# Leftover columns in four groups of 32 partitions, and the column products of k and k+8 made together

## The chip, the cores and the metric

The kernel runs on one core of one Trainium2 chip. The metric is the device time of one execution in microseconds, the median of several runs. An execution is recorded by the hardware profiler; the profile is a page of summaries and a trace of single instructions. The engines are PE (TensorE; PEld is its weight load), DVE (VectorE), ACT (ScalarE), POOL (GpSimd) and SP (the queue that issues most DMAs).

## What is computed

```
def _A_ref(x, w_r, w_i):                     # x: 1 x 2048 x 576
    X = rfft2(x, axes=(-2, -1))
    X = X * (w_r + 1j * w_i)                 # w: 2048 x 289
    return irfft2(X, s=(2048, 576)).astype(bfloat16)

def _B_ref(x, w_gate, w_up, w_down):         # 576 x 4608, 4608 x 576
    return (gelu(x @ w_gate) * (x @ w_up)) @ w_down

h  = x + _A_ref(layernorm(x), w_r, w_i)
h2 = h + _B_ref(layernorm(h), w_gate, w_up, w_down)
```

All arrays are bfloat16. The first part is a spectral filter, the second a gated feed-forward network.

## The kernel before

The order of every engine's work is the order in which the program is written (a manual schedule); waits between engines are put in from what each instruction reads and writes. All sums in PSUM share one pool of four slots, each of two banks (`two`), so a product can start only when the slot that it gets has been evicted.

**Row stage.** The 2048 rows lie as 128 partitions times 16 values of h. For each h, DVE makes a 128-point Fourier table that already holds the row's 1/sigma (`norms`, L391: `FR` from `F16` and `rstd`; half of it with plus, half with minus sign). `row16` (L318) multiplies the columns of x with it: columns d and d+288 are added with both signs, so a group of 128 columns gives 128 sums and 128 differences, and a further product with the constant `mneg` takes the mean away. Two groups cover columns 0 to 255 and 288 to 543. The 2 x 32 columns left over, 256 to 287 and 544 to 575, go through `row16_rest` (L347) in two halves of 64 columns, unfolded: 64 x 128 products, two for the data and two for the mean per h, for four h at a time (`rests`). ACT or DVE moves everything from PSUM to `Bt` (`evict`, L361; `evict4`, L367), five groups of 128 partitions by 2048 values: 0 and 2 are sums, 1 and 3 differences, 4 the leftovers. Before the first product, `fill` (L313) runs 12 products of 512 columns whose result is not used. In parallel the Fourier table of the columns, `DT`, is made by POOL, DVE (`phases`, `mirror`) and ACT (`col_sin`); `DF` is a copy of its third group that is zero outside the two leftover strips.

**Column stage.** It runs in turns, one per pair of row frequencies k and k+8, in the order 1, 2, ... 7, 0. `f2(c)` (L543) makes the column products of one of the two, six products of 128 x 290: per parity two on `Bt` and `DT` and one on the leftovers with `DF`. `f2_out` (L560) brings them to SBUF on ACT (`pq`). `f3` (L570) combines the two by eight products, which ACT evicts to `g` and `hs`. DVE adds and subtracts these (`sum_of`, L595), multiplies with the filter's weights (`wmul`, L607: L618 products, L623/L624/L638/L639 sums) and leaves `Zt`; `i3` (L646) makes the way back by ten products per pair, evicted by ACT to `EO`. A turn i holds `f2` of pair i, `f3` of pair i-1, `wmul` of pair i-2 with the sums of pair i-1 inside it, `f2` of the second half of pair i, and `i3` of pair i-3. The loop reads, cut:

```
for i in range(n + 1):
    if not last: f2(order[i]); f2_out(order[i])         # if i != 1
    ...
    f3(order[i-1], 0); f3(order[i-1], 1)
    ...
    wmul(order[i-2], i-1, order[i-1])
    if not last and i: f2(order[i] + 8); f2_out(order[i] + 8)
    ...
    for s in range(3): i3(order[i-3], s)
```

**After it.** `inv_cols` (L703) makes the columns' way back from `EO` with `DQ`, a copy of `DT` in blocks of 58 that `load_dq` (L512) puts together by DMA; `add_rows` (L838) makes the rows' way back, and then comes the feed-forward network: `gate` (L972, products L978) and the down products (L1021, L1040), on weights that SP loads ahead.

Of the kernel before, what the change touches and what calls it, by code (L numbers as in the profile page):

```python
# [20 lines left out]
P = 128  # L21
# [21 lines left out]
def kernel_body(  # L43
# [67 lines left out]
    DF = keep.tile([P, 2, 2, JH], BF16, name="DF")  # L111
# [28 lines left out]
    def minus_means(lo, hi):  # L140
        sh = [P, 2, hi - lo]
        G.tensor_tensor(
            mneg[:, :, lo:hi],
            mv[:, lo:hi, 0].unsqueeze(1).to_broadcast(sh),
            neg[:].unsqueeze(2).to_broadcast(sh),
            ALU.mult,
        )
# [40 lines left out]
    V.memset(DF[:], 0.0)  # L188
# [18 lines left out]
    iota(iD[64:128, 2:3], [[0, 1]], 2 * P + 64 + 192, 1)  # L207
# [103 lines left out]
    FILL = {0: 12}  # L311

    def fill(dst, n):  # L313

        for _ in range(n):
            T.matmul(dst, lhsT=ident[:], rhs=h_sb[:, 0, 0:512], start=True, stop=True)

    def row16(h):  # L318
        if h % 2 == 0:
            ps_f[h] = two("f2t")  # L320
        f2t, b = (ps_f[h], 0) if h in ps_f else (ps_f[h - 1], 1)
        fill(f2t[:, b, :], FILL.get(h, 0))
        x = h_sb[:, h, :]
        plus = FR[:, h, 0:1, :].to_broadcast([P, 2, P])
        for t in range(2):
            for n, d0 in ((0, t * P), (1, DH + t * P)):
                T.matmul(  # L327
                    f2t[:, b, t * 2 * P : (t + 1) * 2 * P],
                    lhsT=x[:, d0 : d0 + P],
                    rhs=FR[:, h] if n else plus,  # L330
                    start=(n == 0),
                    stop=False,
                )
            T.matmul(
                f2t[:, b, t * 2 * P : t * 2 * P + P],
                lhsT=mneg[:, 0, h : h + 1].to_broadcast([P, P]),
                rhs=FR[:, h, 0, :],
                start=False,
                stop=True,
            )  # L340

    def rests(h):
        ps_f["f4", h] = two("f4")
        for i in range(4):
            row16_rest(h + i)

    def row16_rest(h):  # L347
        o = (h % 4) * P
        for mean in (False, True):
            for p0, d0 in ((0, 256), (64, 512)):  # L350
                T.matmul(
                    ps_f["f4", h - h % 4][p0 : p0 + 64, 0, o : o + P],
                    lhsT=mneg[:, 1, h : h + 1].to_broadcast([P, 64]) if mean else h_sb[:, h, d0 : d0 + 64],
                    rhs=FR[:, h, 0, :],
                    start=not mean,
                    stop=mean,
                )
# [8 lines left out]
    def evict4(h):  # L366
        (V.tensor_copy if h >= 8 else A.copy)(  # L367
            Bt[:, 4, :].rearrange("p (c h l) -> p h c l", c=16, h=16)[:, h : h + 4, :, :],
            ps_f["f4", h][:, 0].rearrange("p (h c l) -> p h c l", h=4, c=16),
        )  # L370
# [91 lines left out]
    rests(0)  # L462
# [5 lines left out]
    rests(4)  # L468
# [4 lines left out]
    evict(0, 2)  # L473
    evict4(0)
    evict(4, 6)
    evict4(4)
# [6 lines left out]
    rests(8)  # L483
# [8 lines left out]
    rests(12)  # L492
# [7 lines left out]
    V.tensor_copy(DF[0:32], D3[0:32])  # L500
    V.tensor_copy(DF[96:128], D3[96:128])
    evict4(12)
# [9 lines left out]
    def load_dq(r):  # L512
        for w in range(1 - r, NW):
            j0, j1 = w * JW, (w + 1) * JW
            for lo, hi in ((j0, min(j1, (j0 // P + 1) * P)), ((j0 // P + 1) * P, j1)):
# [27 lines left out]
    def f2(c):  # L543
        ps = two("pq_ps")
        col = slice(slot[c] * P, (slot[c] + 1) * P)
        steps = [(par, t) for par in range(2) for t in (par, par + 2, 4)]
        if c == order[0]:
            steps.sort(key=lambda s: s[1] == 4)
        for par, t in steps:
            T.matmul(  # L550
                ps[:, par, 0:JP],
                lhsT=Bt[:, t, col],
                rhs=DT[:, t // 2, par] if t < 4 else DF[:, par],
                start=(t == par),
                stop=(t == 4),
            )
        pq[c] = wk.tile([P, 2, JP], BF16, name="pq", tag="pq", bufs=6)
        pq_ps[c] = ps
# [541 lines left out]
```

## Time and profile before

| | us |
|---|---|
| median of 3 runs | 494.58 (494.28 to 494.6) |
| profiled execution | 494.6 |
| its span, first to last instruction | 492.8 |
| PE busy | 484.7 (98%) |
| DVE busy | 223.4 (45%) |
| ACT busy | 158.2 (32%) |
| POOL busy | 29.5 (6%) |

The granted TensorE clock is 1.00 throughout. A timeline row has the start in us, the time of one instruction (or of the first to the last end, where "x2" and more are merged), engine, line, operation, what is written and from what, and in brackets how long the engine had been idle before and who released it. Successive instructions of an engine overlap, so the step from start to start is what one costs in a stream, and start plus time is when its result has landed. A window row has a stretch and the busy time of each engine in it.

### The profile page before, as it was taken

What the parts mean: (1) busy time and instruction counts of PE and PEld (TensorE: products, weight loads), DVE (VectorE), ACT (ScalarE), POOL (GpSimd) and SP (SyncE); (2) the same over time, 40 slices, a digit from 0 to 9 for tenths busy, and PEclk for the clock granted to TensorE, in tenths of its full rate; (3) what the DMA queues carried; (4) which work ended last, traced back from release to release, by engine and by line L of the source; (5) the groups of instructions that cost most, each with busy time, mean ns of one, the idle gap of its engine ahead of it and who ended that gap; (6) DMA issues with size and microseconds to landing.
All of it is one profiled execution on the core that took longest, in us unless ns stands there. A gap on an engine that the chain in (4) does not pass through costs nothing.

```text
span 492.8 us, 12868 instructions
## 1 busy us (share of the span) xinstructions
PE 484.7 (98%) x5762; PEld 338.9 (69%) x5762; DVE 223.4 (45%) x457; ACT 158.2 (32%) x280; POOL 29.5 (6%) x84
## 2 busy tenths in 40 slices
PE   6999999999999999999999999999999999999997
PEld 3777789875589955555699755555799655555995
DVE  8999774798622177333311345333121333333111
ACT  8899863322210022332200132332110232232000
POOL 8500010011100011000000000000000000000000
PEclk9999999999999999999999999999999999999999
DMA  8838979769970049966720089876600377760000
GB/s 278 234 74 184 246 115 240 165 128 212 223 161 3 3 118 195 192 145 147 152 65 1 37 170 199 174 145 147 143 3 3 92 158 155 150 146 1 14 13 25
DMA packets 89582, 62.35 MB, mean 127 GB/s; under 512 B 23222, under 2 KB 88118, under 8 KB 89526
## 3 DMA queue, kind: packets, MB, share of 16 engines
q1 hardware_dynamic: 89238, 60.34, 57.5%
q0 software_dynamic: 288, 1.18, 0.7%
q8 instruction: 45, 0.74, 0.7%
q14 instruction: 11, 0.09, 0.1%
HBM read 52.65 MB, written 2.36 MB: 112 GB/s over the span
## 4 chain that ended last, share of the span: by engine, by line
PE 95%; ACT 2%; POOL 1%; DMA 1%; issue 0%; DVE 0%; ACTq 0%; POOLq 0%
PE gu L978 57%; PE acc L1021 27%; PE pq_ps L550 2%; PE cs_ps L709 2%; PE acc L1040 2%; PE eo_ps L658 2%; ACT junk L128 1%; PE y_ps L848 1%; PE gh_ps L568 1%; PE gh_ps L567 1%; DMA h_sb<-in_A_x_dram 1%; POOL rstd L138 1%; ACT Bt L361 0%; POOL wm_r L397 0%; PE eo_ps L682 0%
## 5 line engine op out<-in xcount | busy, mean ns | idle before, releaser
L978 PE MATMUL gu<-Bt,wgu 64*128 64x512 bf16 (+1 forms) x2646 | 270.6, 363 | 0.0
L978 PEld LDWEIGHTS <-wgu 64*128 64x128 bf16 x2646 | 151.5, 94 | 115.6 <-issue 0.3
L987 DVE TENSOR_TENSOR P_sb<-g_sb,gu 128x512 bf16<-128x512 f32 (+1 forms) x156 | 100.4, 645 | 140.3 <-ACT g_sb L986 140.3
L986 ACT ACTIVATE g_sb<-gu 128x512 f32<-128x512 f32 (+1 forms) x156 | 88.0, 564 | 193.5 <-PE gu L978 193.5
L1021 PEld LDWEIGHTS <-P_sb 64*128 64x128 bf16 x2160 | 122.2, 94 | 10.9
L1021 PE MATMUL acc<-wd,P_sb 64*128 64x288 bf16 x1440 | 90.9, 283 | 0.0
L1030 DVE TENSOR_TENSOR part<-part,acc 128x576 f32<-128x576 f32 x15 | 11.3, 754 | 112.6 <-ACT part L1029 112.6
L1029 ACT COPY part<-acc 128x576 f32<-128x576 f32 x15 | 9.6, 639 | 122.8 <-PE acc L1021 122.8
L1021 PE MATMUL acc<-wd_a,P_sb 64*128 64x288 bf16 x720 | 46.8, 283 | 0.0
L550 PE MATMUL pq_ps<-DT,Bt 128*128 128x290 bf16 x64 | 12.3, 286 | 0.7 <-ACT Bt L361 0.7
L978 PE MATMUL gu<-Bt,wgu_e 64*128 64x256 bf16 (+1 forms) x162 | 12.5, 305 | 0.0
L873 DVE TENSOR_SCALAR hrow<-h_sb,mv,rstd 128x1152 bf16<-128x1152 bf16 x14 | 12.2, 868 | 0.6 <-POOL rstd L911 0.6
L138 POOL TENSOR_TENSOR rstd<-rstd,mhalf 128x1 f32<-128x1 f32 (+2 forms) x17 | 12.0, 709 | 1.4
L1032 DVE TENSOR_TENSOR h_sb<-h_sb,part 128x576 bf16<-128x576 bf16 x15 | 11.4, 758 | 0.5
L550 PEld LDWEIGHTS <-Bt 128*128 128x128 bf16 x96 | 9.1, 97 | 3.4 <-ACT Bt L361 0.8
L978 PEld LDWEIGHTS <-wgu_e 64*128 64x128 bf16 x162 | 10.3, 94 | 1.2
L137 POOL TENSOR_SCALAR rstd<-mv 128x1 f32<-128x1 f32 (+2 forms) x17 | 4.1, 242 | 116.7 <-DVE mv L123 116.0
L561 ACT CAST pq<-pq_ps 128x580 bf16<-128x580 f32 x16 | 10.5, 666 | 1.2 <-PE pq_ps L550 1.1
L709 PE MATMUL cs_ps<-DQ,EO 58*128 58x290 bf16 x144 | 10.8, 283 | 0.0
L327 PE MATMUL f2t<-FR,h_sb 128*128 128x256 bf16 x64 | 9.2, 273 | 0.6 <-DVE FR L391 0.6
L709 PEld LDWEIGHTS <-EO 58*128 58x128 bf16 x160 | 7.8, 94 | 2.4 <-issue 0.7
L550 PE MATMUL pq_ps<-DF,Bt 128*128 128x290 bf16 x32 | 8.9, 285 | 0.0
(149 smaller groups left out, 283.9 us busy)
## 6 DMA issues: line engine op xcount, KB each, us to landing
wgu<-in_B_w_gate_dram SPq DMA_DIRECT2D x46, 432.0 KB, 5.1
wgu<-in_B_w_up_dram SPq DMA_DIRECT2D x46, 432.0 KB, 6.1
wd_a<-in_B_w_down_dram SPq DMA_DIRECT2D x1, 1728.0 KB
wd<-in_B_w_down_dram SPq DMA_DIRECT2D x1, 1728.0 KB
wd<-in_B_w_down_dram SPq DMA_DIRECT2D x6, 288.0 KB, 7.9
out_dram<-h_sb SPq DMA_DIRECT2D x3, 576.0 KB
h_sb<-in_A_x_dram SPq DMA_DIRECT2D x4, 288.0 KB, 4.3
h_sb<-in_A_x_dram SPq DMA_DIRECT2D x2, 576.0 KB
```

What stands on the lines that cost most here:

```text
L138: G.tensor_tensor(dst[:, sl], dst[:, sl], mhalf[:, sl], ALU.pow)
L550: T.matmul(ps[:, par, 0:JP], lhsT=Bt[:, t, col], rhs=DT[:, t // 2, par] if t < 4 else DF[:, par], start=(t == par), stop=(t == 4),)
L561: copy(pq[c][:, rs].rearrange("p r (j a) -> p r j a", a=2), pq_ps[c][:, :, 0:JP].rearrange("p a (r j) -> p r j a", r=2)[:, rs],)
L658: T.matmul(pv[:, n], lhsT=z[:, a, w].rearrange("p b j -> p (b j)"), rhs=TI[:, ts[k], 1 - a : 3 - a, :], start=(a == 0), stop=(a == 1),)
L709: T.matmul(ps[:, e, 0:JP], lhsT=EO[x][rows, w, 2 * g : 2 * g + 2].rearrange("p h e k l -> p (h e k l)"), rhs=DQ[rows, w] if w or e else DT ...
L873: V.tensor_scalar(hrow[:], h_sb[:, h, :].rearrange("p (r k) -> p r k", k=64).unsqueeze(2).to_broadcast([P, NR, 2, 64]), mv2[:, h, 0:1], rs ...
L978: T.matmul(gu[:, c, 0:n], lhsT=w[rows, r, i * P : (i + 1) * P], rhs=hl[tcnk % 2][rows, r, lo:hi], start=(r == 0), stop=(r == NR - 1),)
L986: A.activation(g_sb, gu[:, 0, 0:n], ACT.Gelu_apprx_tanh)
L987: V.tensor_tensor(p_sb(f)[:, lo:hi], g_sb, gu[:, 1, 0:n], ALU.mult)
L1021: T.matmul(accs[i][:, c, 0:DH], lhsT=p_sb(f)[rows, st * P : (st + 1) * P], rhs=wd[f // NWA][rows, f % NWA, c * DH : (c + 1) * DH], start=( ...
L1030: V.tensor_tensor(part, part, accs[1][:, :, 0:DH], ALU.add)
L1032: V.tensor_tensor(hv, hv, part, ALU.add)
```

## The change

The leftover columns are folded like the others: each 32 columns of sums and differences, for even and odd c, become a group of 32 partitions of `Bt[:, 4]`, with 64 values per h where there were 128 (c and c+8 lie in different groups). Per h there are ten products of 32 x 64 for four of 64 x 128, and `rests` does eight h at a time, after rows 4 to 7 and after rows 14 and 15; two evictions take the place of four. `DF` goes. `f2(k)` makes k and k+8 together: eight full products, then four on the leftovers that read 32 partitions each, one for each half and parity. Both `f2_out` follow it, ahead of `f3` of the pair before (in turn 1 after it). The long `cosine` in turn 2 moves ahead of `wmul`. The third group of `DT` now holds the same 32 rows four times; its rows 288 and 289, which `DQ` needs, are written by three small ACT operations to the free half of `Bt[:, 4]` (`edge`) and fetched by one more DMA in `load_dq`. `mneg` keeps one of its two rows, and `fill` runs 44 products of 140 columns.

```diff
-    neg = keep.tile([P, 2], FP32, name="neg")
-    for i in range(2):
-        V.memset(neg[:, i : i + 1], -2.0 + i)
-    mneg = keep.tile([P, 2, H], BF16, name="mneg")
+    mneg = keep.tile([P, H], BF16, name="mneg")
...
-    DF = keep.tile([P, 2, 2, JH], BF16, name="DF")
+    edge = Bt[0:2, 4, 8 * P : 8 * P + 4 * JH].rearrange("p (r a j) -> p r a j", r=2, a=2)
...
-        sh = [P, 2, hi - lo]
-        G.tensor_tensor(
-            mneg[:, :, lo:hi],
...
+        G.tensor_scalar(mneg[:, lo:hi], mv[:, lo:hi, 0], -2.0, None, op0=ALU.mult)
...
-    V.memset(DF[:], 0.0)
+    for t, b in ((edge[:, 0, 0], hpib), (edge[:, 0, 1], nhpib), (edge[:, 1].rearrange("p a j -> p (a j)"), zerob)):
+        A.activation(t, zerob[0:2].to_broadcast(list(t.shape)), ACT.Sin, bias=b[0:2])
...
-    iota(iD[64:128, 2:3], [[0, 1]], 2 * P + 64 + 192, 1)
+    for p0 in (32, 64, 96):
+        iota(iD[p0 : p0 + 32, 2:3], [[0, 1]], 2 * P, 1)
...
-    FILL = {0: 12}
+    FILL = {0: 44}
...
-            T.matmul(dst, lhsT=ident[:], rhs=h_sb[:, 0, 0:512], start=True, stop=True)
+            T.matmul(dst[:, 0:140], lhsT=ident[:], rhs=h_sb[:, 0, 0:140], start=True, stop=True)
...
-    def rests(h):
-        ps_f["f4", h] = two("f4")
-        for i in range(4):
-            row16_rest(h + i)
-
-    def row16_rest(h):
-        o = (h % 4) * P
-        for mean in (False, True):
-            for p0, d0 in ((0, 256), (64, 512)):
-                T.matmul(
-                    ps_f["f4", h - h % 4][p0 : p0 + 64, 0, o : o + P],
-                    lhsT=mneg[:, 1, h : h + 1].to_broadcast([P, 64]) if mean else h_sb[:, h, d0 : d0 + 64],
-                    rhs=FR[:, h, 0, :],
-                    start=not mean,
-                    stop=mean,
-                )
+    def rests(h0):
+        ps = ps_f["f4", h0] = two("f4")
+        for h in range(h0, h0 + 8):
+            o = (h - h0) * 64
+            F = FR[:, h].rearrange("p s (x e n) -> p s x e n", x=2, e=2)
+            for n in range(3):
+                for e in range(2):
+                    for par in range(1 if n == 2 else 2):
+                        p0 = 64 * e + 32 * par
+                        T.matmul(
+                            ps[p0 : p0 + 32, 0, o : o + 64],
+                            lhsT=mneg[:, h : h + 1].to_broadcast([P, 32])
+                            if n == 2
+                            else h_sb[:, h, 256 + DH * n : 288 + DH * n],
+                            rhs=F[:, par if n == 1 else 0, :, e],
+                            start=(n == 0),
+                            stop=(n == 2 - par),
+                        )
...
     norms(0, 4)
-    rests(0)
...
     norms(4, 8)
-    rests(4)
+    rests(0)
...
-    evict(0, 2)
+    evict(0, 2, 4, 6)
     evict4(0)
-    evict(4, 6)
-    evict4(4)
...
     norms(8, 12)
-    rests(8)
...
     norms(14, 16)
-    rests(12)
+    rests(8)
...
     evict4(8)
-    V.tensor_copy(DF[0:32], D3[0:32])
-    V.tensor_copy(DF[96:128], D3[96:128])
-    evict4(12)
...
+        p0 = 64 * r + DH % JW
+        nc.sync.dma_start(DQ[p0 : p0 + 2, NW - 1], edge[:, r])
...
-    def f2(c):
...
+    def f2(k):
+        cc = (k, k + 8)
+        for c in cc:
+            ps = pq_ps[c] = two("pq_ps")
+            for par in range(2):
+                for t in (par, par + 2):
+                    T.matmul(
+                        ps[:, par, 0:JP],
+                        lhsT=Bt[:, t, slot[c] * P : (slot[c] + 1) * P],
+                        rhs=DT[:, t // 2, par],
+                        start=(t == par),
+                        stop=False,
+                    )
+            pq[c] = wk.tile([P, 2, JP], BF16, name="pq", tag="pq", bufs=6)
+        for e, c in enumerate(cc):
+            col = (slot[c] // 8 * 4 + slot[c] % 4) * P
+            for par in range(2):
+                rows = slice(64 * e + 32 * par, 64 * e + 32 * par + 32)
+                T.matmul(
+                    pq_ps[c][:, par, 0:JP],
+                    lhsT=Bt[rows, 4, col : col + P],
+                    rhs=D3[rows, par],
+                    start=False,
+                    stop=True,
+                )
...
             f2(order[i])
             if i != 1:
                 f2_out(order[i])
+                f2_out(order[i] + 8)
         if i == 0:
-            f2(order[0] + 8)
-            f2_out(order[0] + 8)
...
             if i == 1:
                 f2_out(order[1])
+                f2_out(order[1] + 8)
...
                     cosine(slice(2, 3))
+                    cosine(slice(3, 9))
...
-        if not last and i:
-            f2(order[i] + 8)
-            f2_out(order[i] + 8)
-            if i == 2:
-                cosine(slice(3, 9))
```

More of the change, by code (lines that the diff above doesn't have):

```diff
@@ L140, in minus_means @@
     def minus_means(lo, hi):
-        sh = [P, 2, hi - lo]
-        G.tensor_tensor(
-            mneg[:, :, lo:hi],
-            mv[:, lo:hi, 0].unsqueeze(1).to_broadcast(sh),
-            neg[:].unsqueeze(2).to_broadcast(sh),
-            ALU.mult,
-        )
+        G.tensor_scalar(mneg[:, lo:hi], mv[:, lo:hi, 0], -2.0, None, op0=ALU.mult)
     def normalise(eng, dst, m, r, h):
@@ L335, in row16 @@
                 f2t[:, b, t * 2 * P : t * 2 * P + P],
-                lhsT=mneg[:, 0, h : h + 1].to_broadcast([P, P]),
+                lhsT=mneg[:, h : h + 1].to_broadcast([P, P]),
                 rhs=FR[:, h, 0, :],
@@ L366, in evict4 @@
     def evict4(h):
-        (V.tensor_copy if h >= 8 else A.copy)(
-            Bt[:, 4, :].rearrange("p (c h l) -> p h c l", c=16, h=16)[:, h : h + 4, :, :],
-            ps_f["f4", h][:, 0].rearrange("p (h c l) -> p h c l", h=4, c=16),
+        (V.tensor_copy if h else A.copy)(
+            Bt[:, 4, 0 : 8 * P].rearrange("p (c h l) -> p h c l", c=8, h=H)[:, h : h + 8],
+            ps_f["f4", h][:, 0].rearrange("p (h c l) -> p h c l", h=8, c=8),
         )
@@ L514, in load_dq @@
             j0, j1 = w * JW, (w + 1) * JW
-            for lo, hi in ((j0, min(j1, (j0 // P + 1) * P)), ((j0 // P + 1) * P, j1)):
+            for lo, hi in ((j0, min(j1, (j0 // P + 1) * P)), ((j0 // P + 1) * P, min(j1, DH))):
                 if lo < hi:
@@ L541, in kernel_body @@
     slot = {k + 8 * e: 8 * x + 4 * e + i for k, (x, i) in place.items() for e in range(2)}
-    def f2(c):
[L544 to L558, printed above, removed]
+    def f2(k):
[23 more added lines that the diff above has]
+                )
     def f2_out(c, copy=A.copy, rs=slice(0, 2)):
```

1 line of the change is left out of this document (removed).

## The prediction

> **What bounds the kernel now.** I read the page's chain first, then busy time by stretch, then each engine's timeline.
>
> ```profile
> PE 95%; ACT 2%; POOL 1%; DMA 1%; issue 0%; DVE 0%; ACTq 0%; POOLq 0%
> 66.00:492.00 426.00, 423.79 (x5081) 292.89 (x5075) 163.32 (x284) 98.85 (x175) 10.82 (x26) 1.00 0.56 117
> 34.64:38.21 3.57, 3.57 (x32) 2.92 (x31) 3.57 (x9) 3.57 (x7) 0.00 (x0) 1.00 0.37 82
> ```
>
> In the two window rows the columns after the length are PE, PEld, DVE, ACT, POOL, then clock and DMA. From 66 us on PE works 423.8 of 426 us and the change touches nothing there, so whatever the stage before it gains or loses arrives at the end whole. That stage runs in turns of 3.57 us, one per column pair k, k+8, and in a turn PE, DVE and ACT are all full. The chain names PE alone; the timelines say why that is not enough.
>
> ```profile
> 28.17 0.76 DVE L618 TENSOR_TENSOR m<-xab,WI 128x1156 bf16<-128x1156 bf16 x1
> 28.84 0.46 DVE L600 TENSOR_TENSOR xab<-g,hs 128x578 bf16<-128x578 bf16 x1
> ...
> 34.27 0.46 DVE L639 TENSOR_TENSOR Zt<-zb,za 128x580 bf16<-128x580 bf16 x1
> 34.64 0.76 DVE L618 TENSOR_TENSOR m<-xab,WR 128x1156 bf16<-128x1156 bf16 x1
> ```
>
> DVE issues two products (0.67 us each, 28.17 to 28.84) and six sums (0.37 each, 34.27 to 34.64): 2 x 0.67 + 6 x 0.37 = 3.56, its whole turn. It is a train without a gap, so less work on PE can't shorten a turn. What counts is when the train leaves, and whether something holds it up.
>
> ```profile
> 22.98 1.38 ACT L561 CAST pq<-pq_ps 128x580 bf16<-128x580 f32 x2 [1.07 <-PE pq_ps L550]
> 24.34 1.04 ACT L278 ACTIVATE TF<-pr,pib 128x896 bf16<-128x896 int32 x1
> 25.29 0.62 ACT L589 CAST g<-gh_ps 128x578 bf16<-128x578 f32 x1
> 25.82 1.79 ACT L561 CAST pq<-pq_ps 128x580 bf16<-128x580 f32 x3
> 27.62 0.64 ACT L589 CAST g<-gh_ps 128x578 bf16<-128x578 f32 x1
> 28.16 0.65 ACT L589 CAST hs<-gh_ps 128x578 bf16<-128x578 f32 x1
> ```
>
> The place to watch is the second turn: hs of pair 2 lands at 28.16 + 0.65 = 28.81, and DVE takes it at 28.84, just when its product is out. There is no slack at all.
>
> **Part 1, the opening.** Gone from DVE: the clearing of DF and neg. Added: three small ACT operations for `edge`, two more iotas on POOL.
>
> ```profile
> 2.81 0.40 ACT L218 ACTIVATE fs<-mu,npib 128x128 f32<-128x128 int32 x1 [0.80 <-DVE mu L216]
> 3.70 0.68 ACT L128 ACTIVATE junk<-h_sb 128x576 bf16<-128x576 bf16 x1 [0.48 <-DMA h_sb<-in_A_x_dram]
> 5.98 0.46 DVE L384 BATCH_NORM_STATS2 st<-h_sb 128x6 f32<-128x288 bf16 x1 [0.52 <-DMA h_sb<-in_A_x_dram]
> 4.05 5.14 PE L316 MATMUL f2t<-h_sb,ident 128*128 128x512 bf16 x12
> 7.57 1.06 POOL L138 TENSOR_TENSOR rstd<-rstd,mhalf 128x4 f32<-128x4 f32 x1
> 9.47 0.82 DVE L391 TENSOR_SCALAR FR<-F,rstd 128x256 bf16<-128x256 bf16 x4
> 9.76 0.38 PE L327 MATMUL f2t<-FR,h_sb 128*128 128x256 bf16 x2 [0.57 <-DVE FR L391]
> ```
>
> All of it is covered: ACT waits 0.80 and 0.48 us there, DVE 0.52 us for x, and three operations under 0.40 each exceed the ACT gap by 0.4 at most; POOL's factors land at 8.63 and DVE takes them at 9.47, room for several iotas. The filler goes from 12 x 512 = 6144 to 44 x 140 = 6160 columns, so it ends as before at 9.2, 0.57 before its follower is released. If each short one took 0.15 instead of 5.14 / 6144 x 140 = 0.117, it would end at 10.65, 0.9 late; the wait for the factors of 19.10 in part 2 swallows that. I take nothing. SP gets one more DMA of two rows in each `load_dq`, first read at the end of the stage: nothing.
>
> **Part 2, the leftovers in the row stage.**
>
> ```profile
> 11.89 0.22 PE L334 MATMUL f2t<-FR,mneg 128*128 128x128 bf16 x1
> 12.04 0.25 PE L351 MATMUL f<-FR,h_sb 128*64 128x128 bf16 x2
> 12.12 0.22 PE L351 MATMUL f<-FR,mneg 128*64 128x128 bf16 x2
> ...
> 12.46 0.22 PE L351 MATMUL f<-FR,mneg 128*64 128x128 bf16 x2
> 12.61 0.39 PE L327 MATMUL f2t<-FR,h_sb 128*128 128x256 bf16 x2
> ...
> 12.90 0.38 PE L327 MATMUL f2t<-FR,h_sb 128*128 128x256 bf16 x2
> ```
>
> A block for four h is 16 products in eight pairs, six steps from 12.12 to 12.46, so 0.057 a pair. 128 columns take 0.057 alone too (0.29 for 640 columns from 12.61 to 12.90), so two halves of the array run side by side. Going into the split array costs 12.04 - 11.89 - 0.057 = 0.09, coming out 12.61 - 12.46 - 0.057 = 0.09. Before: four blocks of 8 x 0.057 + 0.18 = 0.64. After: two blocks, each of 80 products in 24 rounds of up to four side by side. No row shows a round of 64 columns: at the least half a pair's time, 0.0285, so 0.68 + 0.18 = 0.86 a block; at the most, short of one by one, a pair's, 1.37 + 0.18 = 1.55. I work with 0.86, since in the rows above the columns set the time. The block for h 0 to 7 now stands behind rows 4 to 7 on PE, and its eviction behind theirs on ACT; the rows wait less for banks, which brings nothing, as DVE's factors come no earlier.
>
> ```profile
> 19.10 0.48 DVE L391 TENSOR_SCALAR FR<-F,rstd 128x256 bf16<-128x256 bf16 x2
> 19.98 1.93 ACT L361 CAST Bt<-f2t 128x1024 bf16<-128x1024 f32 x2
> 20.54 0.68 DVE L367 CAST Bt<-f 128x512 bf16<-128x512 f32 x1
> ...
> 21.77 0.69 DVE L367 CAST Bt<-f 128x512 bf16<-128x512 f32 x1
> 22.50 1.15 DVE L245 SCALAR_TENSOR_TENSOR pr<-q,s2p,ks 128x896 int32<-128x896 f32 x1
> 21.96 0.67 PE L550 MATMUL pq_ps<-DT,Bt 128*128 128x290 bf16 x4 [0.68 <-ACT Bt L361]
> ```
>
> The last rows wait for DVE's factors at 19.10, then for ACT's last eviction (19.98 + 1.93 = 21.91), and the column products start at 21.96. Neither moves: rows end near 20.5, the second block by 21.4. DVE loses an eviction and two copies, but its one eviction left waits for that block: it ends near 22.2 instead of 22.46, a gain of 0.3 for DVE that ACT takes back in part 3. With rounds of 0.057 the first block is 0.7 longer, ACT's evictions follow it, and the stage starts 0.7 late.
>
> **Part 3, the column products.** Before, c takes six products; after, a pair takes eight full ones, then four small ones on 32 rows each, in four banks, together.
>
> ```profile
> 35.08 1.25 PE L658 MATMUL eo_ps<-TI,Zt 128*128 128x256 bf16 x10
> 36.17 0.41 PE L550 MATMUL pq_ps<-DT,Bt 128*128 128x290 bf16 x2
> 36.41 0.28 PE L550 MATMUL pq_ps<-DF,Bt 128*128 128x290 bf16 x1
> 36.54 0.41 PE L550 MATMUL pq_ps<-DT,Bt 128*128 128x290 bf16 x2
> ```
>
> Three products step by 0.37, one by 0.1235. Before: 12 x 0.1235 = 1.48 a turn. After: 8 x 0.1235 + 0.09 + 0.12 + 0.09 = 1.29. PE gains 0.19 a turn, 1.5 in eight, in a place where DVE does not let it through. Now the order. `f2` makes both halves before `f2_out` can take either, and both now stand ahead of g and hs on ACT. Step by step, by the rows above: products from 21.96 to 22.95, switch to 23.04, small ones land 0.28 later, 23.34; ACT evicts pair 1 at 23.40 and 23.94 (0.535 each, as 25.29 to 25.82; before from 22.98), the sine at 24.47, g at 25.42, pair 2 at 25.95 and 26.49, free at 27.02. Pair 3 needs two of the four bank pairs: by the banks that the built program gives them, the first is that of g (landed 26.04), the second that of the eviction at 25.95 (landed 26.61). So its products run 26.10 to 26.59 and 26.66 to 27.15, the small ones land at 27.24 + 0.28 + 0.02 = 27.54. ACT stands still until 27.60, evicts at 27.60 and 28.13, then g of pair 2 at 28.67 and hs at 29.20, landed at 29.85. DVE, ready at 28.84, starts at 29.89: **the train stops for 1.05 us**. Half of it is the eviction of column 11 that now precedes g and hs (0.535), half the wait for the banks and for the other half's products; behind the waiting eviction stand g and hs on ACT, and behind them DVE. The long cosine moves ahead of `wmul` on ACT, and between the hs of pairs 2 and 3 there lie one eviction and it as before, so the third turn has no stop of its own.
>
> After that a loop over two turns is as long as the train: Zt lands, i3 1.09, the next pair's products 0.99 + 0.09, landing 0.28, two evictions 1.07, g 0.53, hs 0.66, four handovers of 0.05 (21.91 to 21.96), 4.91 in all; then DVE's five steps from the sum to the next Zt, 5 x 0.37 + 0.46 = 2.31. 7.22 against 2 x 3.57 = 7.14: some 0.25 more over six turns. PE gives back about 0.2 at the tail, because before it ran behind Zt (34.27 + 0.46 = 34.73, its i3 at 35.08). Sum: 1.05 + 0.25 - 0.2 = **+1.1 us**. The profiled execution took 494.6 (span 492.8 and 1.8 around it), beside a median of 494.58: 495.7. A measurement of this kernel can tell about 0.2%, 1.0 us.
>
> **Rivals.**
>
> *Small products one by one.* If each small product takes its own slot, at the 0.0285 that products of a pair average, a block is 80 x 0.0285 + 0.18 = 2.5 instead of 0.86: both blocks lie in PE's order ahead of the column products, and after the first has used up the wait at 19.10 they start near 23.8, +1.9. With part 3: +3.1, 497.7. The pairs show two side by side, not that a product's slot can be shorter than 0.0285. Chance 0.1; rounds of 0.057 (+1.8, 496.4) 0.15. The Trainium skill, TensorE: Matmul & The Clock Gate (Part 1, on the floors), says that starts never come closer than about 25 ns however few the columns: taken for every product, 80 would need an estimated 2.0 us a block. Its Part 3 (measured speedup) has neighbouring tiles start some 4 ns apart, which would allow the short rounds; the rows' average of 0.0285 agrees with both.
>
> *The stop is milder.* If the evictions or banks leave pair 3 free earlier, only the order of ACT costs: 0.535, 495.1. For it: 1.79 for three evictions shows small waits in the present order that may go. Chance 0.15.
>
> *Faster: PE sets the turn,* as the chain's 95% says, and DVE only keeps step with it. Then 0.19 a turn is won, 1.5 in eight: 493.1. It decides if hs of pair 2 lands before 28.8, so that there is no stop. Against it stand the DVE rows without a gap: if they hold, no more can be won than DVE's 0.3 of part 2. Chance 0.1.
>
> *The four small column products don't run together:* 4 x 0.12 for 0.12, PE's turn is 3.57 - 1.48 + 1.65 = 3.74, 0.17 over DVE's for six turns, and 0.4 at the stop: +2.5, 497.1. They differ in rows and in banks, which speaks against it; I count it in the 0.15 of the longer rounds.
>
> **Numbers.** Forecast 0.5: 495.7, own range 495.2 to 496.2. The range to the other cases: 494.4 to 497.9. Slower by over 0.2% means above 495.57: 0.33 of the forecast's 0.5 and the 0.25 of slow small products, 0.58; faster 0.08 of the faster case; the rest, 0.34, within.
>
> **What would show it.** In the changed profile: ACT idle before an L560 eviction near 27.0 for about 0.5 us, with PE pq_ps as releaser; DVE idle near 28.9 for about 1 us, released by hs; turns of 3.57 to 3.65; the first block of 80 products in 0.86 us. Wrong if DVE runs through 29 without a stop, if the column products start well after 22, or if anything after 66 us changes its length.

## The result, and the profile after

The changed kernel takes 497.13 us (median of 6 runs, 495.81 to 497.5) beside 494.49 (6 runs, 494.28 to 494.83): 1.005 times the time before, 95% interval 1.0037 to 1.0063. That is 2.6 us more. The forecast was 1.1 more, in a range of 494.4 to 497.9: the direction was right and the range held, the size was not right, and one step of the prediction is wrong. The profiled execution took 497.2, its span is 495.4; the granted clock is 1.00 as before. Lines of the changed kernel stand 1 to 11 lower than those before (L344 is the small products of `rests`, L539 and L551 the full and the small column products, L560 `f2_out`, L588 the evictions to g and hs, L617 the products of `wmul`, L973 the gate products).

The chain of the changed kernel, and the feed-forward network in a window from its first product to its last, first after, then before (stretch, then busy PE, PEld, DVE, ACT, POOL):

```profile
PE 94%; ACT 2%; DMA 1%; DVE 1%; issue 1%; SPq 0%; ACTq 0%
67.65:491.85 424.20, 424.20 (x5093) 295.75 (x5087) 163.28 (x283) 99.36 (x177) 10.78 (x26) 1.00 0.61 117
37.02:40.69 3.67, 3.62 (x32) 2.48 (x30) 3.67 (x10) 3.53 (x7) 0.00 (x0) 1.00 0.22 46
```

```profile
65.31:489.50 424.19, 424.19 (x5092) 293.52 (x5087) 163.37 (x283) 99.42 (x177) 10.82 (x26) 1.00 0.57 117
```

The network has the same length to 0.01 us; a turn of the column stage, 37.02 to 40.69, is 0.10 longer. DVE looks as full in it as before, but the row counts an instruction as busy while the next could already overlap it: the step from the second product of `wmul` to the sum behind it (37.69 to 38.45) is 0.76 where it was 0.67 (28.17 to 28.84), because that sum reads hs, which landed at 38.43. "issue" has come up from 0% to 1% of the chain: time in which an engine waited for nothing that the profile shows. The marks of the two traces, in us:

| | before | after | later by | of that new |
|---|---|---|---|---|
| first column product (PE) | 21.96 | 23.30 | 1.34 | +1.34 |
| first product of `wmul` (DVE) | 27.49 | 28.93 | 1.44 | +0.10 |
| second | 31.07 | 33.45 | 2.38 | +0.94 |
| seventh | 48.92 | 51.51 | 2.59 | +0.21 |
| first gate product (PE) | 65.31 | 67.65 | 2.34 | -0.25 |
| last DMA to the output issued | 490.31 | 492.65 | 2.34 | 0.00 |
| end of the span | 492.8 | 495.4 | 2.6 | +0.26 |

The largest entry is the first, and it is made in the row stage. Timeline of the changed kernel there, PE and PEld, then POOL, then ACT:

```profile
14.77 0.24 PE L344 MATMUL f<-FR,h_sb 128*32 128x64 bf16 x8
...
15.36 0.19 PE L344 MATMUL f<-FR,mneg 128*32 128x64 bf16 x1
15.95 0.19 PE L344 MATMUL f<-FR,mneg 128*32 128x64 bf16 x1 [0.40 <-issue]
15.97 0.22 PE L344 MATMUL f<-FR,h_sb 128*32 128x64 bf16 x2
16.69 0.26 PE L344 MATMUL f<-FR,h_sb 128*32 128x64 bf16 x6 [0.51 <-issue]
...
16.90 0.39 PE L320 MATMUL f2t<-FR,h_sb 128*128 128x256 bf16 x2
...
21.39 0.24 PE L344 MATMUL f<-FR,h_sb 128*32 128x64 bf16 x8
...
22.07 0.20 PE L344 MATMUL f<-FR,mneg 128*32 128x64 bf16 x2
23.30 1.16 PE L539 MATMUL pq_ps<-DT,Bt 128*128 128x290 bf16 x8 [1.02 <-ACT Bt L356]
24.39 0.30 PE L551 MATMUL pq_ps<-DT,Bt 32*128 32x290 bf16 x4
24.62 1.16 PE L539 MATMUL pq_ps<-DT,Bt 128*128 128x290 bf16 x8
15.33 0.10 PEld L344 LDWEIGHTS <-mneg 128*32 128x32 bf16 x2
15.38 1.09 POOL L392 DMA_INDIRECT wm_i<-in_A_w_i_dram,rev  x1 [0.18 <-issue]
17.07 0.58 ACT L362 CAST Bt<-f 128x512 bf16<-128x512 f32 x1 [1.19 <-PE f L344]
18.21 2.11 ACT L356 CAST Bt<-f2t 128x1024 bf16<-128x1024 f32 x2 [0.56 <-PE f2t L327]
...
21.33 1.91 ACT L356 CAST Bt<-f2t 128x1024 bf16<-128x1024 f32 x2
```

The second block of 80 small products runs from 21.39 to 22.07 without a stop, 0.0086 us a product. The first starts as fast, and then PE stands still twice, from 15.36 to 15.95 and from 15.99, the second product of the row at 15.97, to 16.69. The weights of the product that comes at 15.95 were loaded at 15.33 (PEld x2), and no engine is named as releaser. The first block so lasts 14.77 to 16.90, 2.13 us instead of the 0.86 of the forecast. From there it is handed down: rows 8 to 11 start at 16.90 (before: 15.48), ACT stands idle for 1.19 and 0.56 us, its last two evictions start at 21.33 instead of 19.98, and the column products wait for them until 23.30. On POOL one thing lies beside both holes, the issue of the second gather of the filter's weights, 15.38 to 16.47.

Now the train, DVE and then ACT:

```profile
29.61 0.76 DVE L617 TENSOR_TENSOR m<-xab,WI 128x1156 bf16<-128x1156 bf16 x1
31.21 0.47 DVE L599 TENSOR_TENSOR xab<-g,hs 128x578 bf16<-128x578 bf16 x1 [0.84 <-ACT hs L588]
...
33.45 0.76 DVE L617 TENSOR_TENSOR m<-xab,WR 128x1156 bf16<-128x1156 bf16 x1
28.90 1.19 ACT L560 CAST pq<-pq_ps 128x580 bf16<-128x580 f32 x2 [0.43 <-PE pq_ps L551]
29.97 0.66 ACT L588 CAST g<-gh_ps 128x578 bf16<-128x578 f32 x1
30.50 0.68 ACT L588 CAST hs<-gh_ps 128x578 bf16<-128x578 f32 x1
```

This is the stop of the prediction, 1.34 later: ACT idle 0.43 before the evictions of pair 3, released by the small column products, g and hs behind them, and DVE without work from 30.37 to 31.21.

### The profile page after: what moved, and what is told of

The parts are those of the page before. It is cut to its first block, busy times and chain, and to the rows that moved or that the text cites. A ratio compares the mean times of both kernels' runs of the same rounds, so it can differ in the third digit from the quotient of the medians.

```text
span 495.4 us, 13123 instructions
## 1 busy us (share of the span) xinstructions
PE 484.0 (98%) x5890; PEld 341.3 (69%) x5890; DVE 222.4 (45%) x451; ACT 158.7 (32%) x282; POOL 29.5 (6%) x86
## 4 chain that ended last, share of the span: by engine, by line
PE 94%; ACT 2%; DMA 1%; DVE 1%; issue 1%; SPq 0%; ACTq 0%
PE gu L973 57%; PE acc L1016 27%; PE cs_ps L708 2%; PE acc L1035 2%; PE eo_ps L657 2%; PE pq_ps L539 1%; DMA h_sb<-in_A_x_dram 1%; PE y_ps L843 1%; PE f2t L320 1%; ACT pq L560 1%; PE gh_ps L566 1%; PE gh_ps L567 1%; ACT Bt L356 0%; DVE st L379 0%; PE pq_ps L551 0%
## 5 line engine op out<-in xcount | busy, mean ns | idle before, releaser
L973 PE MATMUL gu<-Bt,wgu 64*128 64x512 bf16 (+1 forms) x2646 | 270.6, 363 | 0.0
L973 PEld LDWEIGHTS <-wgu 64*128 64x128 bf16 x2646 | 152.7, 94 | 114.4 <-issue 0.3
L973 PE MATMUL gu<-Bt,wgu_e 64*128 64x256 bf16 (+1 forms) x162 | 12.5, 305 | 0.0
L973 PEld LDWEIGHTS <-wgu_e 64*128 64x128 bf16 x162 | 10.4, 94 | 1.1
L539 PE MATMUL pq_ps<-DT,Bt 128*128 128x290 bf16 x64 | 9.3, 286 | 1.3 <-ACT Bt L356 1.0
L560 ACT CAST pq<-pq_ps 128x580 bf16<-128x580 f32 x16 | 9.5, 651 | 2.4 <-PE pq_ps L551 1.9
L657 PE MATMUL eo_ps<-TI,Zt 128*128 128x256 bf16 x70 | 8.8, 273 | 1.1 <-ACT pq L560 0.9
L657 PEld LDWEIGHTS <-Zt 128*128 128x128 bf16 x70 | 6.3, 97 | 3.7 <-issue 1.6
```

The costliest lines, as they stand in the source:

```text
L539: T.matmul(ps[:, par, 0:JP], lhsT=Bt[:, t, slot[c] * P : (slot[c] + 1) * P], rhs=DT[:, t // 2, par], start=(t == par), stop=False,)
L560: copy(pq[c][:, rs].rearrange("p r (j a) -> p r j a", a=2), pq_ps[c][:, :, 0:JP].rearrange("p a (r j) -> p r j a", r=2)[:, rs],)
L657: T.matmul(pv[:, n], lhsT=z[:, a, w].rearrange("p b j -> p (b j)"), rhs=TI[:, ts[k], 1 - a : 3 - a, :], start=(a == 0), stop=(a == 1),)
L973: T.matmul(gu[:, c, 0:n], lhsT=w[rows, r, i * P : (i + 1) * P], rhs=hl[tcnk % 2][rows, r, lo:hi], start=(r == 0), stop=(r == NR - 1),)
```

## The experiments

Two questions: what makes the holes (1.34 us), and what makes the stop and the rest of the column stage (1.0 us). The kernel before ran beside every version, with medians of 494.46 to 494.66. The edits are shortened, and remarks behind # in them are not in the kernels. From trace to trace the first row product comes between 9.33 and 10.15 us, whatever the edit, so lengths are compared inside one trace (it comes at 9.76 and 9.78 in the two traces above).

**Did PE run out of instructions?** The first theory on the holes (S): the 32 additional filler products and the 80 small ones use up instructions faster than they come. Two versions, one that takes the additional instructions away and one that adds more of them to the kernel before.

```diff
-    FILL = {0: 44}
+    FILL = {0: 12}
...
-            T.matmul(dst[:, 0:140], lhsT=ident[:], rhs=h_sb[:, 0, 0:140], start=True, stop=True)
+            T.matmul(dst, lhsT=ident[:], rhs=h_sb[:, 0, 0:512], start=True, stop=True)
```

> The changed kernel with the filler as it was, 12 products of 512 columns instead of 44 of 140; all else is the changed kernel. In the changed kernel's trace the first block of 80 small products lasts from 14.77 to 16.90 us, with two holes of 0.40 and 0.51 us in it that wait for nothing the trace shows (issue), while the second block has none and lasts from 21.39 to 22.2. Theory S (supply): PE ran out of instructions; the hole comes behind its 165th product, and the trace has one 16 KB packet of the instruction queue at 16.3 us in both kernels. With 32 products fewer ahead of the block its 80 products end at about the 145th, before the supply is out: no hole, block 0.8 to 0.9 us, column products start at 22.0 instead of 23.30, kernel 1.3 us shorter than the change, 495.8. Theory B (block): something in the block itself, or in the transfers beside it at 15.4 to 16.7 us, stops PE: the holes stay where they are, 497.1.

Measured: 497.15. Timeline, PE and POOL:

```profile
15.72 0.24 PE L344 MATMUL f<-FR,h_sb 128*32 128x64 bf16 x3 [0.37 <-issue]
16.46 0.24 PE L344 MATMUL f<-FR,h_sb 128*32 128x64 bf16 x5 [0.50 <-issue]
15.18 1.09 POOL L392 DMA_INDIRECT wm_i<-in_A_w_i_dram,rev  x1 [0.17 <-issue]
```

The holes stayed, within one product at the same place of the block, though 32 products fewer had gone before. S in this form falls. In the changed kernel, too, the instruction packet starts at 16.34 and takes 1.08 us, and PE goes on at 16.69, before it is through.

```diff
-    FILL = {0: 12}
+    FILL = {0: 110}
...
-            T.matmul(dst, lhsT=ident[:], rhs=h_sb[:, 0, 0:512], start=True, stop=True)
+            T.matmul(dst[:, 0:56], lhsT=ident[:], rhs=h_sb[:, 0, 0:56], start=True, stop=True)
```

> The kernel before with its filler cut into 110 products of 56 columns (6160 columns for 6144); all else is the kernel before, with no block of small products. Theory S: the 165th product is now the 67th of the trace before, among the rows of h 4 to 7 at about 13.7 us: PE stops there, with issue as the cause, until instructions come (at the latest with the packet near 16.3 us), so a hole of 0.5 to 3 us in a stretch of ordinary products; what of it reaches the column products (they start at 21.96 before) makes the kernel 0.3 to 2.5 us longer, 494.8 to 497. Theory B: no hole, 494.5.

Measured: 494.59, 1.0002 times before (0.9993 to 1.0011), and no hole put down to issue among the row products. Both versions also say that the filler's new form costs nothing.

**The gather.** In both traces with holes the gather moved along with them. Three versions tell it from the length of the block and from the transfers.

```diff
     minus_means(8, 12)
-    gather(1)
...
     minus_means(14, 16)
+    gather(1)
     norms(12, 14)
```

> The changed kernel with the second gather of the W table (wm_i, on POOL at 15.38 to 16.47 us) moved behind the last factors on POOL, to about 19 us. The two holes in the first block of 80 products, from 15.36 to 16.69, lie just over this gather in the changed kernel and in its version with the old filler, where both stand 0.2 earlier. Theory G (gather): the products stall while POOL issues the gather: holes gone, block 0.8 to 0.9 us, column products at about 22.0, kernel 1.3 us below the changed one, 495.8. Theory Q (rate): 69 products at 0.009 us each outrun something that feeds or drains PE: holes as they were, 0.59 us into the block, 497.1. Theory T (transfers): the packets of the first gather, wm_r, on the software queue from 14.6 to 16.2 us: holes as they were, 497.1.

Measured: 496.02, 1.0026 times before (1.0012 to 1.0041): 1.1 below the changed kernel. Timeline, PE and POOL:

```profile
14.62 0.24 PE L344 MATMUL f<-FR,h_sb 128*32 128x64 bf16 x8
...
15.30 0.20 PE L344 MATMUL f<-FR,mneg 128*32 128x64 bf16 x2
19.08 1.10 POOL L392 DMA_INDIRECT wm_i<-in_A_w_i_dram,rev  x1 [0.16 <-issue]
```

Both blocks run through, the first in 14.62 to 15.30, and the column products start at 21.82. Theory Q falls. So does T: the packets of wm_r run beside the first block as they did before (48 packets of the software queue between 14.62 and 15.31), and it has no hole.

```diff
     norms(4, 8)
-    rests(0)
...
     evict(0, 2, 4, 6)
-    evict4(0)
...
     norms(8, 12)
+    rests(0)
...
     evict(8, 10)
+    evict4(0)
```

> The changed kernel with the first block of 80 products moved behind the row products of h 8 to 11, to about 17.5 us, and its eviction behind theirs. Without a hole the column products would start at about 22.2 and the kernel take 495.9. Theory G: POOL issues no gather then: no hole. Theory T: the packets of wm_r are through by 16.2: no hole from them; those of the second gather run then. Theory Q: the block is as long and as fast as before, and the holes come again 0.59 us after its first product: block about 2.1 us, column products at 23.3 or later, 497.2.

Measured: 496.19 (1.0034, 1.002 to 1.0049), block from 17.65 to 18.33 without a hole, column products at 22.24: moving the block away from the gather does what moving the gather does.

```diff
-        for h in range(h0, h0 + 8):
-            o = (h - h0) * 64
+        for h in range(h0, h0 + 4):
+            o = h % 8 * 64
...
     norms(0, 4)
+    rests(0)
...
     norms(4, 8)
-    rests(0)
+    rests(4)
...
     norms(8, 12)
+    rests(8)
...
     norms(14, 16)
-    rests(8)
+    rests(12)
```

> The changed kernel with its 160 small products in four runs of 40, each behind the row products of its four h as in the kernel before, two runs to one bank and eviction. Theory Q: no run is longer than 40 products, under the 69 after which the hole came: no hole, rows and blocks as the prediction had them, column products at 21.7 to 22.0, kernel 1.3 to 1.5 us below the changed one, 495.6 to 495.8. Theory G: the first run lies at 12.0 us beside the first gather (11.78 to 13.01): a hole there, hidden in part by the wait for DVE's factors to 12.48; the run at 14.9 ends before the second gather starts. Theory T: the run at 14.9 meets the packets, hole of 0.5 or more there, 496.5 to 497.

Measured: 497.02 (1.0053, 1.0036 to 1.007). Timeline, DVE, PE, POOL:

```profile
12.24 0.97 DVE L388 TENSOR_SCALAR FR<-F,rstd 128x256 bf16<-128x256 bf16 x4
13.15 0.38 PE L320 MATMUL f2t<-FR,h_sb 128*128 128x256 bf16 x2 [0.44 <-DVE FR L388]
...
16.25 0.27 PE L320 MATMUL f2t<-FR,h_sb 128*128 128x256 bf16 x1
16.79 0.27 PE L320 MATMUL f2t<-FR,h_sb 128*128 128x256 bf16 x1 [0.27 <-issue]
11.89 1.23 POOL L394 DMA_INDIRECT wm_r<-in_A_w_r_dram,rev  x1 [0.20 <-ACT junk L125]
15.50 1.09 POOL L394 DMA_INDIRECT wm_i<-in_A_w_i_dram,rev  x1 [0.18 <-issue]
```

Runs of 40 do not help, because both gathers now meet one. Behind the run of 12.18 to 12.5 the next row product comes at 13.15, 0.91 after its factors started on DVE at 12.24; in the changed kernel that step is 0.36 (12.12 to 12.48). The profile puts the wait down to DVE, but it ends 0.03 after the first gather (11.89 + 1.23 = 13.12). Behind the run of 15.44 to 15.8 there is a hole from 16.25 to 16.79 in ordinary row products, ending 0.20 after the second gather (16.59). G is borne out in the cause and missed the place: the second run lay beside the gather too. A hole can also fall on ordinary products, but in every trace with one a run of small products was going on or had just gone.

The reverse: put the gather over the second block, which had no hole in any version. Nine clearings on POOL ahead of it were too many.

```diff
-    gather(1)
...
     minus_means(14, 16)
+    for _ in range(9):                                  # 5 in the last version
+        G.memset(Zts[0][:].rearrange("p a w b j -> p (a w b) j")[:, :, JW:], 0.0)
+    gather(1)
```

> The reverse of the gather moved away: in the changed kernel the second gather is moved on POOL behind the last factors and behind nine more clearings of the pads of one Zt tile (0.16 us each), so that POOL issues it from about 20.5 to 21.6 us, beside the second block of 80 products (20.45 to 21.2 where the gather did not touch it). Theory G: the first block runs through in 0.7 to 0.8 us, and the second block, which had no hole in any kernel so far, now has one or two that end near the end of the gather, 21.6 to 21.9; it lasts 1.2 to 1.5 us. Theory H (the first block has the hole for a reason of its own, and moving the gather changed something else): second block 0.8 us without a hole. The whole time tells little here, since wm_i lands 1.5 us later than in the earlier move and the second product of wmul may wait for it: 496 to 498.

Measured: 501.16 in two runs, and no answer: the gather came at 21.25, after the block's last product at 21.04. The nine clearings (18.77 to 21.09 on POOL) lay beside the whole block, and it had no hole, so the clearings do not make one. The version also shows the price of a late gather: by the profile's waits DVE stood 3.8 us in one piece before its second product of `wmul`, the first that needs these weights.

> As the version before it with the gather late, but with five clearings instead of nine ahead of the gather. Nine put it at 21.25 us, behind the second block (20.36 to 21.05); none at 19.08, ahead of it; five should put it at about 20.3 to 21.4, over the second block. Theory G: the second block, and it alone, now has a hole with issue as its cause, and its last product comes within 0.3 us of the end of the gather, near 21.4 to 21.7 instead of 21.05. Theory H (the first block's own reason): second block 0.7 us, no hole. The column products follow only if the block ends after 21.7; the time as a whole is lengthened by the late wm_i as in the version with nine, 498 to 501.

Measured: 496.24 in one run, beside 494.53. Timeline, PE and POOL:

```profile
21.08 0.22 PE L344 MATMUL f<-FR,h_sb 128*32 128x64 bf16 x3
21.81 0.24 PE L344 MATMUL f<-FR,h_sb 128*32 128x64 bf16 x5 [0.51 <-issue]
20.49 1.10 POOL L392 DMA_INDIRECT wm_i<-in_A_w_i_dram,rev  x1 [0.17 <-issue]
```

Now the second block has the hole, 21.10 to 21.81, and the first has none. No DMA packet starts between 21.10 and 21.81, so what lies beside the hole is the issue on POOL and no transfer. The total was expected too high: DVE did wait 0.52 us for the late weights, but just ahead of its stop for hs, which became shorter by it, so that the second turn lasts 4.51 (27.96 to 32.47) as in the changed kernel (4.52). With this trace the cause is shown from both sides: take the gather off the block and the hole goes, put it on another block and the hole comes there.

The control: the same move in the kernel before, which has no holes.

```diff
     minus_means(8, 12)
-    gather(1)
...
     minus_means(12, 14)
+    gather(1)                  # earlier than above: there DVE waited 0.28 us for wm_i
```

> Control: the kernel before with the second gather moved behind the factors of h 12 and 13 on POOL, nothing else. Its trace shows no hole beside the gather at 15.28 to 16.41. If the 1.1 us that the changed kernel won by the move came from the holes in its small products, nothing is to be won here: 494.3 to 494.7. If the move is worth something by itself (earlier factors, transfers in another order), this kernel is up to 1.1 us faster than before: 493.4.

Measured: 494.77, 1.0011 times before (1.0000 to 1.0022). By itself the move brings nothing that can be measured; what it won in the changed kernel were the holes.

**The order of the column products.** First the order alone, in the kernel before, then the small products alone, in the old order.

```diff
-            f2(order[i])
-            if i != 1: f2_out(order[i])
-        if i == 0: f2(order[0] + 8); f2_out(order[0] + 8)
+            f2(order[i]); f2(order[i] + 8)
+            if i != 1: f2_out(order[i]); f2_out(order[i] + 8)
...
-        if not last and i:
-            f2(order[i] + 8); f2_out(order[i] + 8)
```

The edit also puts the long `cosine` of turn 2 ahead of `wmul`, as the changed kernel has it.

> The kernel before with only the order of the column products changed: f2 of k and of k+8 one behind the other, both evictions behind them, as the changed kernel has it; twelve full products, the leftovers as before. Theory O (order): the stop of DVE at the second turn comes from the order alone, so the gap between the first two products of wmul grows from 3.58 to about 4.6 us; by the steps of the prediction 1.05 of a stop, the later turns as before or up to 0.3 longer in all, column products start unchanged at 21.96: 495.4 to 495.8. Theory M (small products): the stop comes from the four small products and their mode switches; then the order alone costs 0.3 at the most, 494.5 to 494.8.

Measured: 495.63, 1.002 times before (1.0011 to 1.003). The steps between the first products of `wmul` (DVE):

```profile
28.28 0.77 DVE L618 TENSOR_TENSOR m<-xab,WR 128x1156 bf16<-128x1156 bf16 x1
32.46 0.76 DVE L618 TENSOR_TENSOR m<-xab,WR 128x1156 bf16<-128x1156 bf16 x1
36.03 0.76 DVE L618 TENSOR_TENSOR m<-xab,WR 128x1156 bf16<-128x1156 bf16 x1
39.87 0.76 DVE L618 TENSOR_TENSOR m<-xab,WR 128x1156 bf16<-128x1156 bf16 x1
```

The order costs about 1.1 us without any small product. The stop is spread, though: the second turn is 4.18 long (28.28 to 32.46) and not 4.6, another 0.27 comes two turns later (36.03 to 39.87), and 0.39 comes ahead of the first product (5.92 from the first column product at 22.36, before 5.53), where DVE waits for g.

```diff
-    def f2(k):
-        cc = (k, k + 8)
+    def f2(*cc):
...
-                f2_out(order[i]); f2_out(order[i] + 8)
+                f2_out(order[i])
...
+        if not last and i:
+            f2(order[i] + 8); f2_out(order[i] + 8)
```

The long `cosine` goes back behind `wmul` here, and in the two versions that follow.

> The changed kernel with the column products in the order of the kernel before, one column at a time: four full and two small products of k, its eviction, later those of k+8; rests, filler and the opening as changed. Theory O: the stop at the second turn goes, the gap between the first two products of wmul is 3.6 to 3.8 instead of 4.52; with the two holes in the first block still there, column products at 23.3 and the kernel about 0.9 us below the changed one, 496.2. Theory M: the stop stays, with two switches per column instead of per pair it grows, 497.1 to 497.5.

Measured: 496.88 (1.0046, 1.0032 to 1.006), 0.25 below the changed kernel. The stop went as O has it: the second turn is 3.85 long. But the gain was lost behind it, on PE:

```profile
40.51 1.27 PE L657 MATMUL eo_ps<-TI,Zt 128*128 128x256 bf16 x10
41.62 0.66 PE L538 MATMUL pq_ps<-DT,Bt 128*128 128x290 bf16 x4
42.21 0.29 PE L551 MATMUL pq_ps<-DT,Bt 32*128 32x290 bf16 x2
...
44.25 1.27 PE L657 MATMUL eo_ps<-TI,Zt 128*128 128x256 bf16 x10
```

A column takes 0.59 for its four full products with the way into the small tiles, and 0.23 for its two small ones with the way out, as much as four small ones take in the changed kernel (24.39 to 24.62): going in and out sets that price. 0.82 for 0.74 before, twice a turn, makes PE's turn 3.74 (40.51 to 44.25); DVE runs on in 3.57, and PE comes 0.6 late to the tail. So small products pay only in pairs, and pairs in the new order stop the train.

A middle way is to keep the pairs on PE and give ACT its old order.

```diff
             f2(order[i])
-            f2_out(order[i]); f2_out(order[i] + 8)
+            f2_out(order[i])                            # k + 8 too for i == 0
...
             wmul(order[i - 2], i - 1, order[i - 1])
+        if not last and i:
+            f2_out(order[i] + 8)
```

> The changed kernel with the second gather behind the factors of h 12 and 13, and with the evictions of the column products in the order of the kernel before: k ahead of g and hs of the pair before, k+8 behind them and behind wmul; the products of k and k+8 stay together on PE. Theory O: of the stop at the second turn the half that is the eviction goes (0.535) and the half that is banks and the other half's products stays: gap between the first two products of wmul about 4.0 instead of 4.51, kernel about 0.5 below the one with only the gather moved, 495.4 to 495.6. Theory M (the small products and their switches make the stop): gap stays at 4.5, 496.

Measured: 495.07, 1.0011 times before (1.0002 to 1.002). DVE:

```profile
27.37 0.77 DVE L617 TENSOR_TENSOR m<-xab,WR 128x1156 bf16<-128x1156 bf16 x1
29.16 0.47 DVE L599 TENSOR_TENSOR xab<-g,hs 128x578 bf16<-128x578 bf16 x1 [0.35 <-ACT hs L588]
31.39 0.76 DVE L617 TENSOR_TENSOR m<-xab,WR 128x1156 bf16<-128x1156 bf16 x1
```

The second turn is 4.02 long, with the gather moved alone 4.51: the eviction is worth 0.49 of the stop, and the rest is the wait for the other half's products and banks (ACT still stands 0.43 before it evicts pair 3). The later turns are all 3.57 here, so their +0.21 came from ACT's order too, the eviction or the `cosine`; that is why the kernel takes less than either theory had.

Last, all of it together: gather moved, one column at a time for four turns, pairs with the old evictions for the other four; the negation of G on DVE also moves to an earlier place.

```diff
+    MODES = "HHHHPPPP"                                  # H: as in halves, P: as above
```

> A version made of what was learnt: the changed kernel with the second gather behind the factors of h 12 and 13; the first four turns in the order of the kernel before, one column at a time; from the fifth on the products of k and k+8 together, evictions in the old order; the negated copy of G made while DVE waits for the sine. By the steps found so far: column products at 21.9, no stop of more than 0.3 at the second turn, turns of 3.57, tail as before: 494.4 to 494.9, no difference from the kernel before that a measurement can tell. If small products in column order cost the turn as much as in the version in halves (3.74 on PE), the tail shows it: up to 495.3.

Measured: 494.68, 1.0004 times before (0.9995 to 1.0013). The second turn is 3.67 long, and the tail, from the seventh product of `wmul` to the first gate product, takes 16.22 (before 16.39, changed 16.14). The whole loss is taken back, and nothing is won: no version here beats the kernel before.

## Why the prediction was right, and where it was not

**Part 1, the opening,** was right: the filler's old form changes nothing (497.15), and the rows start at 9.78 instead of 9.76. The new filler itself ended at 9.50 (4.19 + 5.31) and not at 9.2, which the wait for the factors covered.

**Part 2** is the step that failed: "the column products start unchanged". Its price for the blocks was right where nothing disturbs them: 14.62 to 15.30 and 21.39 to 22.07, 0.69 for 24 rounds, 0.0288 a round beside the 0.0285 worked with. The Trainium skill, TensorE: Matmul & The Clock Gate (Part 1) has starts never closer than about 25 ns; 0.0086 us a product here shows that this is no floor for products on different tiles. Part 3 of that page of the Trainium skill, with neighbouring tiles some 4 ns apart, fits better: the eight products of the row at 14.77 span 0.24 us where one alone takes 0.19 (15.36), so their starts lie within 0.05 us. What failed was that the block was costed from PE's rows alone. It lies beside POOL's gather, which had been there in the trace before (15.28 to 16.41) beside row products that it didn't hold up. The first block took 2.13 us instead of 0.86, and the "wait for the factors of 19.10", which was to swallow delays, swallowed none: ACT's evictions come behind the block. The prediction did name this path, as what rounds of 0.057 would do ("the stage starts 0.7 late"), with another cause and half the size. With the gather moved away the step holds: from the first row product to the first column product it is 12.20 us (9.62 to 21.82), as before the change (9.76 to 21.96).

**Part 3** was right nearly to the number. Terms of the sum, forecast and measured: the stop 1.05 and 0.94, the six further turns 0.25 and 0.21 (made in five of them), the tail -0.2 and -0.25, the start of the train 0 and 0.10: 1.1 and 1.0. The pair was put at 1.29 and takes 1.32 (23.30 to 24.62). ACT's idle time was to last from 27.02 to 27.60; it ended at 28.90 after 0.43 us, which is 27.13 to 27.56 when the 1.34 of the late start is taken off. The two halves of the stop, 0.535 for the eviction and 0.5 for banks and products, were 0.49 and 0.44 (4.51 to 4.02, 4.02 to 3.58). With the gather out of the way the changed kernel takes 496.02, 1.4 over before, beside a forecast of 1.1; 0.3 of the 1.4 is the end of the program, below.

That 497.13 lies within the range is in part luck: the range reached so far up, to 497.9, for small products that run slowly, and these were not slow.

**The rivals.** Small products one by one: no (0.69 a block). Rounds of 0.057: no. A milder stop: no. PE sets the turn: no; it has 0.16 a turn less to do (1.32 for 1.48) and the turns did not shorten, and where it got more to do (halves) the turns of DVE did not lengthen, only the tail. Four small column products apart: no, with both switches they take 0.33 (1.32 less 8 x 0.1235).

**After 66 us** nothing was to change its length, and the network did not. But from the issue of the last DMA to the span's end it is 2.5 us before and 2.8 after, in every version built on the changed kernel. The DMA rows of SP's timeline, before and after:

```profile
490.31 0.33 SPq L1048 DMA_DIRECT2D out_dram<-h_sb  x1
```

```profile
492.65 0.33 SPq L1043 DMA_DIRECT2D out_dram<-h_sb  x1
```

In the trace SP ends the program with six waits in the order of the semaphores' numbers, 0.06 us each. Before, that of the last DMA is the sixth; after, it is the first, so five follow it: 0.3 us, from nothing but the numbering. That it is this was read from the traces and not tried.

**What stays open.** Why PE stands while POOL issues an indirect DMA the traces don't show; that the issue holds up PE's supply of instructions is one possibility that no run here tests. The places are regular. In every trace with holes one begins 0.57 to 0.75 us behind the start of a gather and ends 1.26 to 1.31 behind it (15.99 and 16.69 for the gather of 15.38, 21.10 and 21.81 for that of 20.49). The earlier hole, from the gather's start to 0.54 to 0.57 behind it, is there only in the three traces in which a block had run for 0.6 us when the gather began; over the second block, which began 0.19 behind the gather, it is missing. One of the six runs of the changed kernel took 495.81, 1.2 less than the next; whether it had no holes can't be told, since no trace of it was taken.

## What to carry to other kernels

A block of very short products must be costed with what the other engines issue beside it, not from its own rows alone: here the gather's issue on POOL cost nothing beside row products of 0.06 to 0.11 us and 1.3 us beside products of 0.009, and slow ones paid too where fast ones had just gone ahead. Where one engine's work is a train without a gap, a saving on another engine is worth nothing, and the order in which results reach it decides: the same sums cost 1.0 us in one order of products and evictions, and nothing that could be measured in another.

## What the runs showed of the hardware

While POOL issues an indirect DMA, PE can stand still with the next product's weights loaded. In the five traces with holes the last one beside the second gather ends 0.17 to 0.22 us behind the end of that issue (16.47 and 16.69 in the changed kernel, 21.59 and 21.81 where the gather was put on the second block), in blocks of 32-column tiles and once in full products. Splitting the array in four, 80 products of 64 columns take 0.69 us, but going in and out costs about 0.1 each (the first block with the gather moved: 0.09 before 14.62, 0.10 before the next full product at 15.43), so two small products cost what four do (0.23).
